# Attention state held once, scaled on ScalarE and multiplied as two 48x48 products

## The chip, the cores and the metric

The kernel runs on one core of a Trainium2 chip. The metric is device time in microseconds (us) of one execution; lower is better. TensorE is called PE below (PEld its weight loads), VectorE DVE, ScalarE ACT, GpSimd POOL, and SP is the engine that issues the DMAs. Before the change the median is 834.35 us over three runs (833.73 to 834.75).

## What is computed

The reference has three stages, each fed by the one before. Only the first is touched by the change. It is a gated linear attention over 4 batches, 8 heads, 768 tokens and 48 channels per head:

```python
f = 1.0 / (1.0 + np.exp(-f_logit))
state = np.zeros((B, H, D, D), dtype=np.float32)
for t in range(S):
    state = f[:, :, t, :, None] * state + np.einsum('bhd,bhe->bhde', k[:, :, t], v[:, :, t])
    y[:, :, t] = np.einsum('bhd,bhde->bhe', q[:, :, t], state)
```

The other two are a gated layer with a 768x768 mix over tokens (`h = relu(x @ w_in)`, normalize the second half over channels, `w_spatial @ v_n + b_spatial`, gate, `@ w_out`) and a mixer (`u = x + (relu(x.T @ w_tok1) @ w_tok2).T`, `u + relu(u @ w_ch1) @ w_ch2`). Inputs of the attention are of size 0.1 with decay logits around 2; the weights arrive as float64 or float32.

## The kernel before, in words

**Attention.** A unit (`att_unit`) is one pair of heads over half of the tokens of a batch: 4 batches x 2 halves x 4 pairs = 32 units, named batch, half, pair: unit 013 is batch 0, second half, fourth pair. The two heads of a pair lie on partitions 0 to 47 and 64 to 111. A unit has 3 chunks of 128 tokens. `chunked` (L195) works in these steps. ACT makes the decays `fs` by a sigmoid (L346). DVE copies each chunk's first decay into `first` (L202), zeroes it in `fs` (L203), scans the running decay `pc` (L204), bounds the chunk-end decays from below (L209), inverts them (L210), scans the inverse `gc` backwards (L211) and multiplies keys and queries by both (L214). POOL keeps the end decays in `pend` (L207). PE transposes the keys (L220), ACT copies them to `kn` (L222); PE makes the scores of the two heads (L229) into two PSUM tiles `pa`, ACT copies them to `am` (L233), and POOL masks them (L234). PE makes the chunk's sum of keys times values `pk` (L243, L244). DVE keeps the running state `z` of 48 columns (L265, L267), and beside it writes for each chunk but the very first a `state` (L254): `z` scaled by the end decay, set twice side by side into a 112x96 block and multiplied by a mask `own` of ones and zeros, so that the block is diagonal over the two heads. So one product of 112 rows and 112 columns serves both heads (L279); to it are added the values times the masked scores, head by head (L274, L285). There are 80 such states: 2 in each unit of a first half, 3 in each of a second. The result `py` is split into two parts of fewer bits, `xh` (ACT, L357) and `xl` (DVE, L358). The fourth pair's parts, `yh` and `yl`, are copied by 12 small DMAs (L363) into the rows that the others leave.

**Later stages.** `s1` multiplies `xh` and `xl` by w_in (through `mm3`, L130 to L132, PSUM tiles `pv` and `pu`), `s23` makes the mix over tokens (tile `ps`) and the output (`px`), phase 2 the mixer. Weights are split on the chip into two parts, piece by piece, by `split_weight`: a DMA into a ring of three buffers, then steps on DVE (L78, L81, L91), ACT (L85, L87, L92, L98) and POOL (L86, L101).

**Order.** Units are emitted step by step, each unit's first step ahead of the unit before it (`att`), and woven with the steps of `s1`, `s23` and the weights (`weave`). The tile framework then puts the instructions in order with its own scheduler, which knows of every engine, and each engine runs its queue strictly in that order. Loads and the small copies share one DMA-issuing queue, SP's. After the run, `pend`'s least value decides whether a second, general body runs; with these inputs it doesn't.

Of the kernel before, what the change touches and what calls it, by code (L numbers as in the profile page):

```python
# [8 lines left out]
F32 = mybir.dt.float32  # L9
# [9 lines left out]
def tile_kernel(ctx, tc, fkqs, v, w_in, w_sp, b_sp, w_out, w_t1, w_t2, w_c1, w_c2, out):  # L19
# [34 lines left out]
    # weights as sums of two parts of 12 bits each; float64 is rounded to float32 on the way  # L54
    LEAST = 3.4332275390625e-05 ** 2

    def split_weight(pool, stage, src, name, n, cols, eng, first=0, order=None):
        """Tiles of both parts, and the steps that fill them, piece by piece."""
        wide = src.dtype == mybir.dt.uint64
        h = pool.tile([P, n, cols], F32R, name=name + "h")  # L60
        l = pool.tile([P, n, cols], F32R, name=name + "l")
        if wide:
            src = src.bitcast(U32)
        srcr = src.rearrange("(n p) c -> n p c", p=P)

        def piece(i, c0, width):
            sl = (slice(None), i, slice(c0, c0 + width))
            at = stage.tile([P, WST], U32, tag="wsa", name=f"{name}sa{i}{c0}")
            a = at[:, :width]
            if wide:  # L70
                st = stage.tile([P, WST, 2], U32, tag="wst", name=f"{name}st{i}{c0}")
                nc.sync.dma_start(
                    out=st[:, :width, :].rearrange("p c t -> p (c t)"),
                    in_=srcr[first + i][:, 2 * c0 : 2 * (c0 + width)],
                )
                yield
                lo, hi = st[:, :width, 0], st[:, :width, 1]
                nc.vector.tensor_scalar(  # L78
                    out=a, in0=hi, scalar1=3, scalar2=0x3FFFFFFF, op0=ALU.logical_shift_left, op1=ALU.bitwise_and
                )  # L80
                nc.vector.scalar_tensor_tensor(  # L81
                    out=a, in0=hi, scalar=0xC0000000, in1=a, op0=ALU.bitwise_and, op1=ALU.bitwise_or
                )
                # the low word's first 3 bits, rounded
                nc.scalar.activation(lo, lo, AF.Copy, scale=2.0**-29)  # L85
                nc.gpsimd.tensor_tensor(out=a, in0=a, in1=lo, op=ALU.add)  # L86
                nc.scalar.activation(f32(hi), f32(hi), AF.Square)  # L87
                yield
                # zero below float32's least normal number
                a = f32(a)  # L90
                nc.vector.scalar_tensor_tensor(out=a, in0=f32(hi), scalar=LEAST, in1=a, op0=ALU.is_ge, op1=ALU.mult)  # L91
                nc.scalar.copy(h[sl], a)  # L92
                yield
            else:
                a = f32(a)
                nc.sync.dma_start(out=a, in_=srcr[first + i][:, c0 : c0 + width])
                yield
                nc.scalar.copy(h[sl], a)  # L98
                yield
                yield  # L100
            eng.tensor_tensor(out=l[sl], in0=a, in1=f32(h[sl]), op=ALU.subtract)  # L101

        where = [(i, c0, min(WST, cols - c0)) for i in range(n) for c0 in range(0, cols, WST)]
        return h, l, [partial(piece, *x) for x in (order(where) if order else where)]

    def staged(pieces):
        """Steps in which each piece is one stage behind the one after it."""
# [10 lines left out]
    def weave(main, *fillers):  # L118
        """Emit the steps of main with those of the others spread evenly before them."""
        for n, m in enumerate(main):  # L120
            for fl in fillers:
                for x in fl[len(fl) * n // len(main) : len(fl) * (n + 1) // len(main)]:
                    x()
            m()

    def mm3(ps, pairs, first=True, **kw):
        """ps += sum over (lh, ll, rh, rl) of (lh + ll)^T (rh + rl) without the product of both low parts."""
# [6 lines left out]
    def body(general):  # L134
        # ---------------- phase 1 pools
# [37 lines left out]
        first, last = (attp.tile([P, W], F32, name=x) for x in ("first", "last"))  # L173
        states = [attp.tile([P, 128], F32, name=f"state{i}") for i in range(4)]
        own = attp.tile([P, 2, D], F32, name="own")
        for t in [first, last, own] + states:
            nc.gpsimd.memset(t, 0.0)
        for j in range(2):
            nc.gpsimd.memset(own[64 * j : 64 * j + D, j, :], 1.0)
# [5 lines left out]
        cnt = {"state": 0}  # L185
# [9 lines left out]
        def chunked(u, b, hf, p, fs, fkq, vt):  # L195
            ki, qi = fkq[:, 1, :], fkq[:, 2, :]
            n0 = hf * NCW
            # decay from the chunk's start, and its inverse (from the chunk's end backwards); both scans pass
            # through all chunks and start anew where the factor is zero and the other operand is not
            pg = at2.tile([P, 2, W], F32, tag="pg", name=f"pg{u}")  # L200
            gc, pc = pg[:, 0, :], pg[:, 1, :]
            nc.vector.tensor_copy(first[:, ::C], fs[:, :W:C])  # L202
# [4 lines left out]
            nc.gpsimd.tensor_copy(pend[:, b * NP + p, n0 : n0 + NCW], pc[:, C - 1 :: C])  # L207
            ends = last[:, C - 1 :: C]
            nc.vector.tensor_scalar(out=ends, in0=pc[:, C - 1 :: C], scalar1=LOW, scalar2=None, op0=ALU.max)  # L209
            nc.vector.reciprocal(ends, ends)  # L210
# [5 lines left out]
            # keys with tokens on partitions  # L216
# [6 lines left out]
            # scores, transposed  # L223
# [15 lines left out]
            # chunk states  # L239
# [7 lines left out]
            for c in range(NCW):  # L247
                n = n0 + c
                if n > 0:
# [4 lines left out]
                    nc.vector.scalar_tensor_tensor(  # L254
                        out=now[c][:112].rearrange("p (j e) -> p j e", j=2)[:, :, :D],
                        in0=zprev[:112].unsqueeze(1).to_broadcast([112, 2, D]),
                        scalar=pp[:112],
                        in1=own[:112],
                        op0=ALU.mult,
                        op1=ALU.mult,  # L260
                    )
# [10 lines left out]
            # only a bank's first product may start afresh; where nothing was written since, the others store  # L272
# [5 lines left out]
            for c in range(now[0] is None, NCW):  # L278
                nc.tensor.matmul(  # L279
                    py[:112, c, :], now[c][:112, :112], qi[:112, c * C : (c + 1) * C],  # L280
                    start=c == 0, stop=False, skip_group_check=True,
                )
# [8 lines left out]
        def scanned(u, b, hf, p, fs, fkq, vt):  # L291
            """The recurrence itself, token by token, for one value channel of both heads after the other."""
# [36 lines left out]
        def att_unit(b, hf, p):  # L329
            """The steps of one pair of heads over half of the tokens."""  # L330
# [18 lines left out]
            # the last pair's channels fill the rows that the others leave  # L349
# [15 lines left out]
        def att(units):  # L365
            """Steps of these units in turn, the first of each ahead of the unit before it."""
# [97 lines left out]
        # ---------------- phase 1  # L464
# [44 lines left out]
        if not general:  # L509
            # does any chunk's decay come near float32's range?  # L510
# [8 lines left out]
        # ---------------- phase 2  # L519
# [70 lines left out]
        def ff(b, hf):  # L590
            """Token half hf through both channel layers; a block's second product comes after the next one's first."""
# [78 lines left out]
    # If so, all is done again in a way that holds for any decay.  # L670
# [47 lines left out]
```

## Time and profile before

| | |
|---|---|
| median of 3 runs (lowest, highest) | 834.35 us (833.73, 834.75) |
| span of the profiled execution | 835.6 us |
| PE busy | 770.3 us, 92% |
| PEld busy | 708.6 us, 85% |
| DVE busy | 462.2 us, 55% |
| ACT busy | 277.7 us, 33% |
| POOL busy | 232.9 us, 28% |

The page gives no time of the profiled execution besides its span, from the first instruction to the last; it is 1.25 us above the median of the runs. A share over the whole span says little here: attention runs in the first 370 us only, beside the loading and splitting of weights at first and beside the products of the later stages after that. In rows of the timeline a matmul's end is modelled, so only starts are subtracted from starts. A float32 product appears as two matmul records, an fp32r product (L130 to L132) as one.

### The profile page before, as it was taken

The page shows a single profiled execution, that of the slowest core. Times are in us where ns is not written, and L with a number is a line of the kernel's source. Part 1 is how long each engine was busy: PE and PEld are TensorE (multiplying, and loading weights), DVE is VectorE, ACT ScalarE, POOL GpSimd, SP SyncE. Part 2 cuts the span into 40 slices and gives each one's busy share as a digit, 9 for nine tenths or more (in the row PEclk, how much of TensorE's full clock was granted, in tenths as well). Part 3 has the DMA queues.
Part 4 walks back from the last instruction along what each step waited for, and adds up shares of the span by engine and source line. Part 5 has one row for each costly group of instructions (what it writes and reads, how often), then busy time and mean ns, then how long its engine had stood idle before and what let it go on. Part 6 is the DMA issues. An engine that isn't in the chain of part 4 may idle for free.

```text
span 835.6 us, 12502 instructions
## 1 busy us (share of the span) xinstructions
PE 770.3 (92%) x4785; PEld 708.6 (85%) x4785; DVE 462.2 (55%) x916; ACT 277.7 (33%) x590; POOL 232.9 (28%) x290
## 2 busy tenths in 40 slices
PE   3579599999999999999879889999999999999996
PEld 2357478988889878998769788999999999999995
DVE  6988977783777648638996796222122312222211
ACT  4544543333423343226645553112111311111110
POOL 5786721121112122106873661004001210001000
PEclk9999679999999999999999999999999999999998
DMA  7464321330223211203434321002000200000001
GB/s 248 128 210 131 127 93 56 129 107 33 86 77 110 91 38 57 90 20 107 153 95 130 128 72 59 21 1 86 1 29 1 86 1 28 1 1 30 14 16 34
DMA packets 30055, 61.09 MB, mean 73 GB/s; under 512 B 4128, under 2 KB 19872, under 8 KB 29984
## 3 DMA queue, kind: packets, MB, share of 16 engines
q1 hardware_dynamic: 29984, 60.18, 22.5%
q8 instruction: 40, 0.66, 0.3%
q14 instruction: 31, 0.25, 0.1%
HBM read 48.37 MB, written 9.44 MB: 69 GB/s over the span
## 4 chain that ended last, share of the span: by engine, by line
PE 71%; DVE 15%; DMA 6%; issue 4%; ACT 1%; POOL 1%; SPq 1%; DVEq 0%; ACTq 0%; POOLq 0%
PE po L615 17%; PE p L132 7%; PE p L131 7%; PE p L130 7%; PE ps L130 4%; PE ps L132 3%; PE ps L131 3%; PE pa L229 3%; PE py L285 2%; PE py L279 2%; PE px L130 2%; PE px L132 2%; PE px L131 2%; PE pv L130 2%; PE pu L130 2%
## 5 line engine op out<-in xcount | busy, mean ns | idle before, releaser
L603 DVE SCALAR_TENSOR_TENSOR hl<-p,hh 128x384 fp32r<-128x384 f32 x96 | 53.4, 557 | 176.5 <-ACT hh L602 176.5
L602 ACT ACTIVATE hh<-p 128x384 fp32r<-128x384 f32 x96 | 47.1, 491 | 183.4 <-PE p L132 183.4
L615 PE MATMUL po<-hl,wc2h 128*128 128x384 f32 x288 | 98.2, 341 | 1.4 <-DVE hl L603 1.4
L615 PE MATMUL po<-hh,wc2l 128*128 128x384 f32 x288 | 97.3, 338 | 0.0
L626 POOL TENSOR_TENSOR us<-uh,ul 128x384 f32<-128x384 f32 x24 | 25.4, 1066 | 197.6 <-DVE ul L586 180.3
L615 PE MATMUL po<-hh,wc2h 128*128 128x384 f32 x288 | 76.0, 340 | 4.0 <-ACT hh L602 4.0
L234 POOL TENSOR_SCALAR_AFFINE_SELECT am<-am 128x384 f32<-128x384 f32 x64 | 40.7, 651 | 114.8 <-ACT am L233 114.7
L130 PE MATMUL ps<-wsph,vh 128*128 128x384 f32 x192 | 67.3, 350 | 1.7 <-DVE g L439 1.7
L132 PE MATMUL ps<-wsph,vl 128*128 128x384 f32 x192 | 65.3, 343 | 0.3 <-DVE vl L412 0.3
L131 PE MATMUL ps<-wspl,vh 128*128 128x384 f32 x192 | 65.2, 340 | 0.0
L132 PE MATMUL p<-uh,wc1l 128*128 128x384 f32 x192 | 64.9, 338 | 0.0
L131 PE MATMUL p<-ul,wc1h 128*128 128x384 f32 x192 | 64.7, 337 | 0.0
L130 PE MATMUL p<-uh,wc1h 128*128 128x384 f32 x192 | 64.6, 338 | 0.1
L615 PEld LDWEIGHTS po<-hh,wc2h 128*128 128x128 f32 x288 | 52.4, 189 | 5.5 <-ACT hh L602 5.5
L615 PEld LDWEIGHTS po<-hl,wc2h 128*128 128x128 f32 x288 | 54.5, 189 | 2.7 <-DVE hl L603 2.7
L615 PEld LDWEIGHTS po<-hh,wc2l 128*128 128x128 f32 x288 | 54.5, 189 | 0.0
L279 PE MATMUL py<-fkq,state 112*112 112x128 f32 x160 | 36.1, 324 | 8.1 <-DVE state L254 6.1
L229 PE MATMUL pa<-fkq 48*128 48x128 f32 x384 | 42.5, 331 | 0.9 <-ACT am L233 0.9
L229 PEld LDWEIGHTS pa<-fkq 48*128 48x128 f32 x384 | 31.9, 217 | 10.8 <-issue 5.4
L130 PEld LDWEIGHTS ps<-wsph,vh 128*128 128x128 f32 x192 | 36.2, 188 | 5.0 <-DVE g L439 2.0
L279 PEld LDWEIGHTS py<-fkq,state 112*112 112x112 f32 x160 | 26.7, 198 | 14.9 <-DVE state L254 9.0
L130 PE MATMUL pu<-xh,winh 128*128 128x384 f32 x96 | 34.6, 361 | 5.0 <-ACT u L419 3.4
(167 smaller groups left out, 1933.6 us busy)
## 6 DMA issues: line engine op xcount, KB each, us to landing
fkq<-in_fkq SPq DMA_DIRECT2D x31, 576.0 KB, 3.8
vt<-in_v SPq DMA_DIRECT2D x8, 576.0 KB, 6.0
x1d<-xs SPq DMA_DIRECT2D x24, 192.0 KB, 1.9
xf<-x1d SPq DMA_DIRECT2D x12, 384.0 KB, 4.5
wc2st<-in_w_c SPq DMA_DIRECT2D x12, 384.0 KB, 3.2
out<-ot SPq DMA_DIRECT2D x24, 192.0 KB, 2.0
wc1st<-in_w_c SPq DMA_DIRECT2D x8, 384.0 KB, 3.8
winst<-in_w_in SPq DMA_DIRECT2D x6, 384.0 KB, 4.1
```

The lines of the kernel that those rows point to most:

```text
L130: nc.tensor.matmul(ps, lh, rh, start=first and i == 0, stop=False, **kw)
L131: nc.tensor.matmul(ps, lh, rl, start=False, stop=False, **kw)
L132: nc.tensor.matmul(ps, ll, rh, start=False, stop=i == n - 1, **kw)
L229: nc.tensor.matmul(pa[j][:, c, :], ki[64 * j : 64 * j + D, sl], qi[64 * j : 64 * j + D, sl], start=True, stop=True)
L234: nc.gpsimd.affine_select(out=am[j], in_=am[j], compare_op=ALU.is_ge, fill=0.0, base=0, pattern=[[0, NCW], [1, C]], channel_multiplier=-1,)
L279: nc.tensor.matmul(py[:112, c, :], now[c][:112, :112], qi[:112, c * C : (c + 1) * C], start=c == 0, stop=False, skip_group_check=True,)
L285: nc.tensor.matmul(py[64 * j : 64 * j + m, c, :], vt[:, c, h0 + D * j : h0 + D * j + m], am[j][:, c, :], start=False, stop=True, skip_grou ...
L602: nc.scalar.activation(hh, ps, AF.Relu)
L603: nc.vector.scalar_tensor_tensor(out=hl, in0=ps, scalar=0.0, in1=f32(hh), op0=ALU.max, op1=ALU.subtract)
L615: nc.tensor.matmul(po[c], l[:, ft, csl], r, start=ft == 0 and x == 0, stop=ft == NF - 1 and x == 2)
L626: nc.gpsimd.tensor_tensor(out=us[c], in0=f32(uh[:, c, tsl]), in1=f32(ul[:, c, tsl]), op=ALU.add)
```

## The change

The state is held once, 48 columns wide, in six tiles of 64 columns whose last 16 stay zero, and is scaled by ACT. The product with the queries becomes two, one for each head, of 48 rows and 64 or 48 columns. The mask `own` goes. `first` has two tiles, and ACT fills it by a sigmoid of the chunk's first logits, beside the one that makes `fs`. `pend` is copied by ACT. The end decays are inverted without the bound from below. Lines after L202 move up by 2 to 9; comments are taken out, which moves nothing.

```diff
-        first, last = (attp.tile([P, W], F32, name=x) for x in ("first", "last"))
-        states = [attp.tile([P, 128], F32, name=f"state{i}") for i in range(4)]
-        own = attp.tile([P, 2, D], F32, name="own")
-        for t in [first, last, own] + states:
+        firsts = [attp.tile([P, W], F32, name=f"first{i}") for i in range(2)]
+        last = attp.tile([P, W], F32, name="last")
+        states = [attp.tile([P, 64], F32, name=f"state{i}") for i in range(6)]
+        for t in firsts + [last] + states:
             nc.gpsimd.memset(t, 0.0)
-        for j in range(2):
-            nc.gpsimd.memset(own[64 * j : 64 * j + D, j, :], 1.0)
...
-            nc.vector.tensor_copy(first[:, ::C], fs[:, :W:C])
+            first = firsts[cnt["unit"] % 2]
+            cnt["unit"] += 1
+            nc.scalar.activation(first[:, ::C], fkq[:, 0, ::C], AF.Sigmoid)
             nc.vector.memset(fs[:, ::C], 0.0)
...
-            nc.gpsimd.tensor_copy(pend[:, b * NP + p, n0 : n0 + NCW], pc[:, C - 1 :: C])
-            ends = last[:, C - 1 :: C]
-            nc.vector.tensor_scalar(out=ends, in0=pc[:, C - 1 :: C], scalar1=LOW, scalar2=None, op0=ALU.max)
-            nc.vector.reciprocal(ends, ends)
+            nc.scalar.copy(pend[:, b * NP + p, n0 : n0 + NCW], pc[:, C - 1 :: C])
+            nc.vector.reciprocal(last[:, C - 1 :: C], pc[:, C - 1 :: C])
...
-                    nc.vector.scalar_tensor_tensor(
-                        out=now[c][:112].rearrange("p (j e) -> p j e", j=2)[:, :, :D],
-                        in0=zprev[:112].unsqueeze(1).to_broadcast([112, 2, D]),
-                        scalar=pp[:112],
-                        in1=own[:112],
-                        op0=ALU.mult,
-                        op1=ALU.mult,
-                    )
+                    nc.scalar.activation(now[c][:112, :D], zprev[:112], AF.Copy, scale=pp[:112])
...
             for c in range(now[0] is None, NCW):
-                nc.tensor.matmul(
-                    py[:112, c, :], now[c][:112, :112], qi[:112, c * C : (c + 1) * C],
-                    start=c == 0, stop=False, skip_group_check=True,
-                )
+                for j, m in ((0, 64), (1, D)):
+                    r = slice(64 * j, 64 * j + D)
+                    nc.tensor.matmul(
+                        py[64 * j : 64 * j + m, c, :], now[c][r, :m], qi[r, c * C : (c + 1) * C],
+                        start=c == 0, stop=False, skip_group_check=True,
+                    )
```

The scheduler then orders each engine's instructions anew. Three places follow.

On PE, unit 110's products of state and queries (its tile `py110`; `ps011` is the mix of batch 0). Before:

```order
L131 MATMUL ps011_1541<-wspl_498,vh0_501 128x384
L279 MATMUL py110_1483<-fkq110_1291,state1_125 112x128
L132 MATMUL ps011_1541<-wsph_497,vl0_502 128x384
L279 MATMUL py110_1483<-fkq110_1291,state2_126 112x128
L285 MATMUL py110_1483<-am1100_1440,vt11_1295 64x128
L285 MATMUL py110_1483<-am1101_1441,vt11_1295 48x128
```

Now:

```order
L132 MATMUL ps011_1559<-wsph_503,vl0_508 128x384
L272 MATMUL py110_1499<-fkq110_1307,state5_130 64x128
L272 MATMUL py110_1499<-fkq110_1307,state5_130 48x128
L130 MATMUL ps011_1559<-wsph_503,vh0_507 128x384
L131 MATMUL ps011_1559<-wspl_504,vh0_507 128x384
L132 MATMUL ps011_1559<-wsph_503,vl0_508 128x384
L272 MATMUL py110_1499<-fkq110_1307,state0_125 64x128
L272 MATMUL py110_1499<-fkq110_1307,state0_125 48x128
L278 MATMUL py110_1499<-am1100_1456,vt11_1311 64x128
```

Where a product of full height stood between other full-height products, two of 48 rows stand between them.

On ACT, the copy of unit 003's result, `yh003`, from which the first DMAs into `xh00` are made (`wsph` is a piece of the mix's weights, `wspsa` its load). Before:

```order
L98 CAST wsph_497<-wspsa20_604 128x384
L98 CAST wsph_497<-wspsa2384_627 128x384
L357 CAST yh003_479<-py003_461 112x384
L98 CAST wsph_497<-wspsa30_655 128x384
L222 COPY kn011_609<-pt011_606 128x224
```

Now:

```order
L98 CAST wsph_503<-wspsa20_610 128x384
L98 CAST wsph_503<-wspsa2384_633 128x384
L252 ACTIVATE state3_128<-z0100_572,pend_64 112x48
L252 ACTIVATE state4_129<-z0101_575,pend_64 112x48
L98 CAST wsph_503<-wspsa30_664 128x384
L350 CAST yh003_485<-py003_465 112x384
```

`yh003` now stands behind the piece `wsph` of the load `wspsa30`, and behind two states.

On ACT, the same copy at the end of batch 0, `yh013` (`wt1st` are loads of w_t1, `vh0` and `u00` tiles of `s1`). Before:

```order
L411 CAST vh0_501<-vf002_765 128x512
L87 ACTIVATE wt1st00_3930<-wt1st00_3930 128x256
L357 CAST yh013_881<-py013_864 112x384
L92 CAST wouth_499<-woutsa30_1101 128x384
```

Now:

```order
L252 ACTIVATE state1_126<-z0131_880,pend_64 112x48
L85 ACTIVATE wt1st10_4004<-wt1st10_4004 128x256
L220 COPY kn100_984<-pt100_980 128x336
L92 CAST wouth_505<-woutsa30_1114 128x384
L231 COPY am1000_988<-pa1000_986 128x384
L231 COPY am1001_989<-pa1001_987 128x384
L207 COPY pend_64<-pg101_972 128x3
L87 ACTIVATE wt1st10_4004<-wt1st10_4004 128x256
L85 ACTIVATE wt1st20_4030<-wt1st20_4030 128x256
L350 CAST yh013_895<-py013_875 112x384
```

Between the state that unit 013's last product needs and the copy of its result there now stand eight instructions, among them the conversion of the load `wt1st20`, which before came after `yh013`.

## Rows read from the trace of the kernel before

**Rows 1.** Windows: stretch in us; its length, busy of PE, PEld, DVE, ACT, POOL; PEclk, DMA

```profile
0.00:62.90 62.90, 33.55 (x234) 25.31 (x234) 53.82 (x106) 29.95 (x67) 43.46 (x60) 1.00 0.63 195
62.90:104.70 41.80, 32.25 (x206) 24.48 (x205) 37.65 (x79) 20.33 (x47) 27.88 (x30) 0.82 0.41 130
104.70:113.40 8.70, 8.69 (x30) 6.74 (x31) 5.87 (x13) 3.54 (x9) 2.22 (x5) 0.50 0.53 174
113.40:370.00 256.60, 256.60 (x1862) 223.04 (x1860) 172.50 (x413) 90.56 (x198) 46.85 (x94) 1.00 0.23 74
370.00:835.00 465.00, 439.22 (x2460) 428.99 (x2458) 192.32 (x308) 133.32 (x271) 112.50 (x101) 0.98 0.15 49
```

**Rows 2.** Chain that ended last, 94 to 106 us: start, us, what

```profile
95.31 0.59 DVE state L254
95.94 0.77 PE py L279 x2
...
98.23 0.48 ACT yh L357
...
99.80 4.78 DMA xh<-yh
...
104.71 0.77 PE pv L130
```

**Rows 3.** Timeline of PE at unit 110's products: start, us, line, tiles, records

```profile
152.25 0.38 PE L279 MATMUL py<-fkq,state 112*112 112x128 f32 x2
152.39 0.42 PE L132 MATMUL ps<-wsph,vl 128*128 128x384 f32 x1
152.66 0.38 PE L279 MATMUL py<-fkq,state 112*112 112x128 f32 x2
152.97 0.87 PE L285 MATMUL py<-am,vt 128*64 128x128 f32 x12
153.76 0.45 PE L130 MATMUL ps<-wsph,vh 128*128 128x384 f32 x1
154.05 0.34 PE L131 MATMUL ps<-wspl,vh 128*128 128x384 f32 x1
154.22 0.35 PE L132 MATMUL ps<-wsph,vl 128*128 128x384 f32 x1
...
155.75 0.94 PE L229 MATMUL pa<-fkq 48*128 48x128 f32 x12
156.90 0.34 PE L131 MATMUL px<-woutl,gh 128*128 128x384 f32 x1
```

**Rows 4.** Timeline of PE, a shorter run of the same products

```profile
122.81 0.65 PE L285 MATMUL py<-am,vt 128*64 128x128 f32 x8
123.39 0.44 PE L130 MATMUL pu<-xh,winh 128*128 128x384 f32 x1
```

**Rows 5.** Groups by line and shape: count, busy us, mean ns, idle before

```profile
L254 DVE SCALAR_TENSOR_TENSOR state<-z,pend,own 112x96 f32<-112x96 f32 x80 | 31.2, 391 | 3.9 <-PE py L279 2.6
L209 DVE TENSOR_SCALAR last<-pg 128x3 f32<-128x3 f32 x32 | 9.6, 301 | 0.7
L202 DVE COPY first<-fs 128x3 f32<-128x3 f32 x32 | 5.7, 177 | 34.8 <-ACT fs L346 34.7
L207 POOL COPY pend<-pg 128x3 f32<-128x3 f32 x32 | 12.0, 376 | 67.4 <-DVE pg L204 67.4
L222 ACT COPY kn<-pt 128x336 f32<-128x336 f32 x16 | 7.0, 434 | 4.5 <-PE pt L220 4.5
L222 ACT COPY kn<-pt 128x224 f32<-128x224 f32 x16 | 5.5, 346 | 10.4 <-PE pt L220 10.4
```

**Rows 6.** Timelines of SP and ACT at the first copies into xh

```profile
54.14 0.33 SPq L96 DMA_DIRECT2D wspsa<-in_w_sp  x1
...
54.62 0.47 ACT L357 CAST yh<-py 112x384 fp32r<-112x384 f32 x1
56.56 0.51 ACT L98 CAST wsph<-wspsa 128x384 fp32r<-128x384 f32 x1 [1.46 <-DMA wspsa<-in_w_sp]
```

More of the change, by code (lines that the diff above doesn't have):

```diff
@@ L184, in body @@
             nc.gpsimd.memset(pick[64 : 64 + D, D + 64 : D + 65], 1.0)
-        cnt = {"state": 0}
+        cnt = {"state": 0, "unit": 0}
         zst = {}
```

## The prediction

> **What bounds the kernel now.** I read the windows by stage first, then the chain of waits, then the timeline of PE. The windows [rows 1] show three stages in which attention runs. Up to 62.9 us DVE is busy 53.8 us and PE 33.6: DVE's queue carries the start. From 62.9 to 104.7 DVE is busy 37.7 of 41.8 and PE 32.3, so DVE still leads. From 104.7 to 370 PE has work in every microsecond, at half the granted clock up to 113.4 and at the full one after. The reader should see that the 55% of DVE over the span says nothing: DVE matters only before 104.7, PE only after. The chain [rows 2] shows how the one hands over to the other: a state by DVE at 95.31, the product that waits for it at 95.94, ACT's copy of unit 013's result at 98.23, its DMAs into `xh` (4.78 us), and the first product of `s1` on batch 0's second half at 104.71. After that no row of the chain is anything but PE until the attention is done. What comes after 370 is not touched; its weight buffers take the room of the attention's, so it starts as much earlier or later as the attention ends.
>
> So the change takes work from DVE, which pays only before 104.7, and asks PE for more, which costs only after. The two have to be weighed.
>
> **PE after 104.7: the products.** In this stretch stand 58 of the 80 products of state and queries. One now costs 0.23 us: from 152.25 to 152.66 are 0.41, with one full-size product of about 0.175 in it [rows 3]. In its place come two of 48 rows, each of two records. Nothing in the trace is a product of 48 rows into 64 columns. Nearest above: each of the two costs what the one cost, 0.23, as if they ran one after the other; that adds 58 x 0.23 = 13.3 us. Nearest below: one record's 0.0525 for each of the two passes, the heads side by side, 0.105 in all, which saves 58 x 0.125 = 7.3. I take the rate of the small products: L285 needs 0.79 us for 12 records and 0.58 for 8 [rows 3, 4], so 0.0525 a record and 0.21 for four; L229, the nearest in rows used, has the same rate (below). That is 58 x 0.02 = **1.2 us less**.
>
> **PE after 104.7: the changes of form.** The rows show that full-height products follow each other freely, `L279` between fp32r products too, but that a change to a small form costs. L285 starts 0.31 us after L279, which is 0.08 over its 0.23. Its 12 records take 0.79 for 0.63 at the steady rate, 0.16 more, and the second full-size product starts 0.29 after the first where 0.17 is usual [rows 3]. The run of 8 has the same 0.16 over its 0.42 [rows 4]. I put 0.05 of it on the way in and 0.11 on the way out: 0.13 for a change into a 64-column form, 0.22 for one into a full form. The run of L229 takes 1.15 us from its first record to the second full-size product; less 0.63 for its records and 0.17 that leaves 0.35, of which 0.22 are the way out; with an entry like L285's 0.08 ahead of it a change into the 48-row, 128-column form costs 0.20 to 0.21.
>
> I counted the changes in PE's order from the first product at 104.7 to the attention's last. Before: 84 into a full form, 38 into L229's, 57 into 64 columns, 179 in all. Now: 76, 52 and 105, of which 44 are into the new form; 233 in all. The reason is the first place shown of the order: a product that stood among full ones without a toll now pays twice. At 0.22, 0.20 and 0.13 that is 33.5 us before and 40.8 now, **7.3 more**. (The same counting with all products at their steady rates gives 257 us for the stretch, where the trace has 265, 4.4 of them lost to the half clock, so it holds to some 2%.) In the new order 2 full-size products, 6 score products and some 9 small ones of this stretch stand ahead of it, while PE waits for the DMAs; at 0.17, 0.11 and up to 0.07 each that is **1.6 less**. Sum for PE: 7.3 - 1.2 - 1.6 = **+4.5 us**.
>
> A rule speaks against the products. The Trainium skill, "TensorEngine Tiling (Array Packing)", section "Restrictions and Gotchas", has it that different row tiles cannot access the same PSUM bank at the same time. Here both heads write one bank, while the pair of L229 writes two tiles; no row shows row tiles on one bank. By the rule the sum would take the upper price, +13.3 in place of -1.2.
>
> **DVE, ACT and POOL.** DVE loses L254 (391 ns), L209 (301) and L202 (177) [rows 5]. Before 104.7 these are 22, 10 and 11 instructions, 8.6 + 3.0 + 1.9 = 13.5 us; that is the most that the start can gain, and nothing is the least. After 104.7 they are hidden behind PE and are worth nothing. POOL loses 32 copies of 376 ns, some 10 of them before 104.7; POOL is busy 43.5 of the first 62.9 us, so this helps the weight pieces a little and I give it nothing of its own. ACT gets 64 instructions of 3 columns and 80 of 48. Its copies of 336 and 224 columns take 434 and 346 ns, so 0.17 us and 0.8 ns a column: 0.17 and 0.21. Before 104.7 that is some 8 us beside 50 busy ones of 104.7: room enough, but each stands in a queue that runs in order. `first` now waits for ACT where it waited for DVE, at like cost.
>
> **How much of the 13.5 arrives.** Two places of the order decide it. At the first copies into `xh00`, SP issues a load at 54.14, ACT copies `yh003` at 54.62 and turns the load that was just issued at 56.56 [rows 6]. Now `yh003` stands behind that piece. If the loads go out 3.5 us sooner, because POOL's pieces follow DVE's, the piece ends at 57.07 - 3.5 and the copy 0.5 later, at 54.1, against 55.1: one microsecond of gain, not five. At the end of the half the same happens. DVE reaches unit 013's last state some 3 us sooner by its shorter queue, and ACT makes it without DVE's other work in between, so the product at 95.94 comes to about 91. But `yh013` now waits for `wt1st20`. That load needs a buffer which DVE's last piece of w_out frees right after the state, at about 91.5; a load takes 2.4 us from issue to ACT in [rows 6], this larger one say 3.2, and its 256 columns 0.4 on ACT, so `yh013` starts at about 95.2 against 98.23. So I take **3.0 us** of gain at 104.71, an estimate from these rows, between the ends of 0 and 13.5.
>
> **Sum.** +4.5 - 3.0 = +1.5 us. The profiled execution's span of 835.6 would become 837.1; it is 1.25 above the median, and the difference is carried over to that: 834.35 + 1.5, rounded up to **836.0 us** for tolls that DVE's relief cannot hide. A measurement of this kernel tells about 0.2% from no change, 1.7 us.
>
> **Rivals.**
> *The start's gain arrives (faster).* If `yh013` does not wait for the load, two thirds of the 13.5 come through, 9 us, against +4.5 on PE: 829.9; all of it gives 825.4. For it: DVE is busy 90% of 62.9 to 104.7 [rows 1]. Against it: both copies stand behind loads. It decides once the first product of `s1`'s second half starts before 100.2. If PE then idles less, the half clock from 104.7 to 113.4 may not come, worth 8.7 / 2 = 4.4 us more.
> *Small forms change freely among themselves (faster).* 55 of the changes now are between the new form and another small one, 49 of them into 64 columns. Without their toll, 49 x 0.13 + 6 x 0.20 = 7.6 us, PE comes to -3.1 and the time to 828. Against it: the run of L229 pays on its way out as L285 does.
> *The two heads run one after the other (slower).* In `py` both write one bank. PE comes to +4.5 + 1.2 + 13.3 = +19.0 and the time to 850.4. It decides if four records take more than 0.3 us. Against it: nothing but the pair of L229, on two banks.
> *Nothing arrives at the start (slower).* The DMAs leave no gain: 838.9.
>
> **How the numbers follow.** Forecast, 832 to 840, with the last rival as its upper half: 0.55, of which 0.30 lies above 836.0, 0.25 within 0.2%. Gain at the start 0.17 and free changes 0.13, both faster. One after the other 0.15, slower, and partly so it lies at 840 to 850. So faster 0.30, same 0.25, slower 0.45. The range takes the two faster cases down to 827 and the slow one up to 846, which leaves out a full gain below and a full serial price above, together 2 in 10.
>
> **What would show it.** In the profile after: DVE without the three groups, some 46 us less; L272 in 320 records. The steps are right if four records of L272 in a row take about 0.21 us, if the first full-size product after them comes 0.3 after the one before it, if PE is busy throughout from the first product of `s1`'s second half (at 101 to 102 us) to the attention's end, and that stretch is 4 to 5 us longer. They are wrong if that first product moves by more than 5 us or not at all, if the tolls are not there, or if PE waits for ACT's states after 113.

## The result, and the profile after

| | before | after |
|---|---|---|
| median (lowest, highest; runs) | 834.39 us (833.73, 834.75; 4) | 845.50 us (843.86, 852.45; 4) |
| ratio, 95% interval | | 1.0147 [1.0107, 1.0187] |
| span of the profiled execution | 835.6 us | 842.4 us |
| PE busy | 770.3 us | 781.2 us, 93% |
| DVE, ACT, POOL busy | 462.2, 277.7, 232.9 us | 430.2, 307.6, 227.7 us |

The kernel became 11.1 us slower: inside the range and on the forecast side, but seven times the forecast's 1.6. The two profiled executions lie only 6.8 us apart, since that of before was one of the slower of its kernel and that of after one of the faster: in the other thirteen traces the span is 1.7 to 1.8 us under the time of its execution, so that of before took an estimated 837.4 us, 3.0 above its median, while that of after took 844.15, 1.35 under its own. So 4.3 of the 11.1 us stand in no trace. The spread of the four runs after, 8.6 us, stays unexplained.

The windows of the changed kernel answer to [rows 1]. Columns: stretch in us; its length, busy of PE, PEld, DVE, ACT, POOL; PEclk, DMA share, GB/s. The stretches are cut at the same places of the program: first product of `s1`, first product of its second half, end of the half clock, end of the attention.

```profile
0.00:61.60 61.60, 33.80 (x257) 23.84 (x257) 47.79 (x82) 35.66 (x98) 42.78 (x54) 1.00 0.64 201
61.60:106.90 45.30, 36.05 (x253) 26.66 (x253) 35.28 (x66) 24.61 (x67) 29.81 (x30) 0.81 0.39 125
106.90:110.20 3.30, 3.30 (x11) 2.46 (x9) 1.24 (x3) 0.58 (x2) 0.00 (x0) 0.50 0.51 135
110.20:378.70 268.50, 268.50 (x1970) 223.77 (x1968) 153.25 (x314) 113.92 (x298) 42.18 (x74) 1.00 0.23 73
```

PE is still busy in every microsecond of the last two. The attention ends 8.7 us later than before, 378.45 against 369.78 by the last product's start, and what follows gives 1.9 back, which no step of the change explains: it takes 463.8 to 467.8 us in the fourteen traces. From the first product of `s1`'s second half to there it was 265.1 us, now it is 271.5; but before, 8.7 of them ran at half clock and now only 3.3. So at full clock it is 260.7 against 269.9: **9.2 us more work on PE**, where 4.5 were forecast. That first product came 2.2 us later, at 106.94, where 3.0 sooner was forecast.

**Where PE's time went.** Timelines of PE, then of its weight loads, at the place of [rows 3], unit 110's products (start, us, line, tiles, records):

```profile
149.99 0.34 PE L132 MATMUL ps<-wsph,vl 128*128 128x384 f32 x1
150.25 0.43 PE L272 MATMUL py<-fkq,state 48*64 48x128 f32 x4
150.61 0.44 PE L130 MATMUL ps<-wsph,vh 128*128 128x384 f32 x1
150.89 0.34 PE L131 MATMUL ps<-wspl,vh 128*128 128x384 f32 x1
...
151.33 0.43 PE L272 MATMUL py<-fkq,state 48*64 48x128 f32 x4
151.69 0.87 PE L278 MATMUL py<-am,vt 128*64 128x128 f32 x12
152.49 0.45 PE L130 MATMUL ps<-wsph,vh 128*128 128x384 f32 x1
```

```profile
149.81 0.19 PEld L132 LDWEIGHTS ps<-wsph,vl 128*128 128x128 f32 x1
150.25 0.19 PEld L272 LDWEIGHTS py<-fkq,state 48*64 48x64 f32 x4 [0.25 <-issue]
150.61 0.19 PEld L130 LDWEIGHTS ps<-wsph,vh 128*128 128x128 f32 x1 [0.17 <-issue]
150.72 0.19 PEld L131 LDWEIGHTS ps<-wspl,vh 128*128 128x128 f32 x1
```

From 149.99 to 150.89 are two full products (0.35 at their steady rate) and one pair of small ones: 0.55 for the pair, where the one product cost 0.23. The weight loads show why. Between products of one form the next weights are loaded while a product runs: L131's at 150.72 under L130's product of 150.61. At a change of form the load stands still for 0.25 or 0.17 us and starts only with the product that needs it. In the rest of the stretch it is the same: before a load that follows one of another form the loads stand still for 0.05 to 0.37 us, 0.17 on the mean of 231, and before one of the same form for at most 0.10 (1714 loads).

The second place is the scores. The rows are PE's timeline after, two units on:

```profile
154.46 0.94 PE L227 MATMUL pa<-fkq 48*128 48x128 f32 x12
155.33 0.44 PE L130 MATMUL px<-wouth,gh 128*128 128x384 f32 x1
...
160.84 0.93 PE L227 MATMUL pa<-fkq 48*128 48x128 f32 x10
161.70 0.65 PE L272 MATMUL py<-fkq,state 48*64 48x128 f32 x8
162.28 0.87 PE L278 MATMUL py<-am,vt 128*64 128x128 f32 x12
163.08 0.49 PE L227 MATMUL pa<-fkq 48*128 48x128 f32 x2
163.49 0.26 PE L241 MATMUL pk<-vt,kn 128*64 128x48 f32 x1
```

A unit's 12 score records take 0.87 us in one piece (154.46 to 155.33). Where the small products break in, 10 take 0.86 and the last 2 another 0.41. Ten cost as much as twelve because a head's product without the other head's beside it takes the time of both: the records of a pair start 7 ns apart and the next pair 0.11 us later, and the last two records of the ten, of one head, start at 161.39 and 161.50. I call such a piece, with an odd number of products, an odd one.

**Where the start went.** PE's timeline around unit 013's product, which answers to [rows 2], and ACT's before its copy:

```profile
93.14 0.68 PE L272 MATMUL py<-fkq,state 48*64 48x128 f32 x4 [2.60 <-DVE xl L351]
94.07 1.28 PE L272 MATMUL py<-fkq,state 48*64 48x128 f32 x8 [0.26 <-ACT state L252]
95.28 1.54 PE L278 MATMUL py<-am,vt 128*64 128x128 f32 x12
...
100.94 0.79 PE L218 MATMUL pt<-ident,fkq 112*128 112x112 f32 x3 [3.50 <-issue]
101.66 1.65 PE L227 MATMUL pa<-fkq 48*128 48x128 f32 x12
...
106.94 0.80 PE L130 MATMUL pv<-winh,xh 128*128 128x512 f32 x1
```

```profile
94.29 0.32 ACT L252 ACTIVATE state<-z,pend 112x48 f32<-112x48 f32 x1
...
97.60 0.20 ACT L207 COPY pend<-pg 128x3 f32<-128x3 f32 x1 [1.16 <-DVE pg L204]
97.91 0.43 ACT L87 ACTIVATE wt1st<-wt1st 128x256 f32<-128x256 f32 x1
98.25 0.42 ACT L85 ACTIVATE wt1st<-wt1st 128x256 uint32<-128x256 uint32 x1
98.57 0.46 ACT L350 CAST yh<-py 112x384 fp32r<-112x384 f32 x1
```

The weight load of the unit's third product, and PE's row of its first product before the change:

```profile
94.67 0.28 PEld L272 LDWEIGHTS py<-fkq,state 48*64 48x64 f32 x4 [0.32 <-ACT state L252]
```

```profile
90.40 0.77 PE L279 MATMUL py<-fkq,state 112*112 112x128 f32 x2 [1.93 <-DVE xl L358]
```

The unit's first product did not wait for its state but, 2.60 us, for DVE to empty `py` of unit 012; it came at 93.14, before the change at 90.40. The second and third, at 94.07 and 94.67, then waited shortly for ACT, which made the last state at 94.29. The copy of their result stood on ACT behind `pend` of unit 101, which now makes ACT wait 1.16 us for DVE's scan, and behind two conversions. Then unit 101's transposes and scores and unit 100's results stand ahead of `s1`'s product on PE, for 6.0 us at half clock.

The new and remaining groups of ACT and PE, as in [rows 5]:

```profile
L252 ACT ACTIVATE state<-z,pend 112x48 f32<-112x48 f32 x80 | 25.7, 332 | 32.7 <-DVE z L258 14.2 <-DVE z L256 9.5 <-PE py L272 7.6
L207 ACT COPY pend<-pg 128x3 f32<-128x3 f32 x32 | 6.3, 196 | 17.7 <-DVE pg L204 17.6
L202 ACT ACTIVATE first<-fkq 128x3 f32<-128x3 f32 x32 | 6.2, 194 | 0.0
L272 PE MATMUL py<-fkq,state 48*64 48x128 f32 x160 | 34.7, 321 | 3.9 <-DVE xl L351 2.6 <-ACT state L252 1.3
L272 PE MATMUL py<-fkq,state 48*48 48x128 f32 x160 | 33.7, 314 | 0.0
```

The three groups of DVE, 46.5 us, are gone, though DVE's busy time fell by only 32.0: records of DVE overlap, and others of them take longer. Of PE's two groups, only 3.9 us of idle time stand ahead, and none of it after 106.9.

### The profile page after: what moved, and what is told of

It reads as the page before. It is cut to its first block, busy times and chain, and to the rows that moved or that the text cites. A ratio compares the mean times of both kernels' runs of the same rounds, so it can differ in the third digit from the quotient of the medians.

```text
span 842.4 us, 12829 instructions
## 1 busy us (share of the span) xinstructions
PE 781.2 (93%) x4945; PEld 707.5 (84%) x4945; DVE 430.2 (51%) x772; ACT 307.6 (37%) x734; POOL 227.7 (27%) x258
## 4 chain that ended last, share of the span: by engine, by line
PE 76%; DVE 11%; issue 4%; DMA 3%; POOL 2%; ACT 1%; SPq 1%; DVEq 0%; POOLq 0%; ACTq 0%
PE po L608 17%; PE p L132 7%; PE p L131 7%; PE p L130 7%; PE ps L130 4%; PE pa L227 4%; PE ps L131 4%; PE ps L132 3%; PE py L272 3%; PE py L278 2%; PE px L130 2%; PE px L132 2%; PE px L131 2%; PE pv L130 2%; PE pv L131 1%
## 5 line engine op out<-in xcount | busy, mean ns | idle before, releaser
L232 POOL TENSOR_SCALAR_AFFINE_SELECT am<-am 128x384 f32<-128x384 f32 x64 | 46.0, 732 | 179.3 <-ACT am L231 179.3
L130 PE MATMUL ps<-wsph,vh 128*128 128x384 f32 x192 | 67.2, 350 | 1.4 <-DVE g L432 1.3
L131 PE MATMUL ps<-wspl,vh 128*128 128x384 f32 x192 | 65.3, 340 | 0.0
L131 PE MATMUL p<-ul,wc1h 128*128 128x384 f32 x192 | 65.1, 339 | 0.0
L130 PE MATMUL p<-uh,wc1h 128*128 128x384 f32 x192 | 64.9, 340 | 0.0
L227 PE MATMUL pa<-fkq 48*128 48x128 f32 x384 | 48.3, 335 | 0.0
L227 PEld LDWEIGHTS pa<-fkq 48*128 48x128 f32 x384 | 35.6, 219 | 12.1 <-issue 8.1
L130 PE MATMUL pu<-xh,winh 128*128 128x384 f32 x96 | 35.1, 366 | 8.2 <-ACT r L390 4.1
L130 PEld LDWEIGHTS ps<-wsph,vh 128*128 128x128 f32 x192 | 36.1, 188 | 5.2 <-issue 1.7
L272 PE MATMUL py<-fkq,state 48*48 48x128 f32 (+1 forms) x320 | 34.7, 317 | 3.9 <-DVE xl L351 2.6
L130 PE MATMUL px<-wouth,gh 128*128 128x384 f32 x96 | 34.4, 360 | 3.5 <-DVE g L432 2.5
```

Of the source, the lines that this page charges most:

```text
L130: nc.tensor.matmul(ps, lh, rh, start=first and i == 0, stop=False, **kw)
L131: nc.tensor.matmul(ps, lh, rl, start=False, stop=False, **kw)
L227: nc.tensor.matmul(pa[j][:, c, :], ki[64 * j : 64 * j + D, sl], qi[64 * j : 64 * j + D, sl], start=True, stop=True)
L232: nc.gpsimd.affine_select(out=am[j], in_=am[j], compare_op=ALU.is_ge, fill=0.0, base=0, pattern=[[0, NCW], [1, C]], channel_multiplier=-1,)
L272: nc.tensor.matmul(py[64 * j : 64 * j + m, c, :], now[c][r, :m], qi[r, c * C : (c + 1) * C], start=c == 0, stop=False, skip_group_check=True,)
```

## The experiments

The kernels built on the change leave out the bound of the end decays, as it does. A product's form is its number of rows (48, or 112 and more) and of columns (64 and less, or 112 and more); with both the larger it is full. "Changes" are changes of form counted in PE's records from the first product of `s1`'s second half to the end of the attention.

**1 to 4: which part of the change costs?** One product with all else of the change (`e1`):

```diff
-                    nc.scalar.activation(now[c][:112, :D], zprev[:112], AF.Copy, scale=pp[:112])
+                    for j in range(2):
+                        r = slice(64 * j, 64 * j + D)
+                        nc.scalar.activation(now[c][r, 64 * j : 64 * j + D], zprev[r], AF.Copy, scale=pp[r])
...
-                for j, m in ((0, 64), (1, D)):
...
+                nc.tensor.matmul(
+                    py[:112, c, :], now[c][:112, :112], qi[:112, c * C : (c + 1) * C],
+                    start=c == 0, stop=False, skip_group_check=True,
+                )
```

> The change with the product put back: ACT writes the two heads' blocks into a 128-column state (two activations in place of one) and one product of 112 rows serves both heads; all that the change moved to ACT stays there. Theory A (the 9 us that PE lost between the first product of s1's second half and the end of the attention come from the small products: more changes of form, and scores of the two heads split from each other by them): in this kernel's order PE changes form 187 times there (179 before, 233 in the change) and 20 pieces of scores hold an odd number of products (14 and 34), so this stretch is 1 to 2 us longer than before, and the time is 833 to 838. Theory B (the loss comes from ACT: states and end decays in its queue, whatever the product): the time stays at 842 to 848, since ACT has 80 more activations still.

Two products in the kernel before (`e2`), the state scaled by DVE:

```diff
-                    nc.vector.scalar_tensor_tensor(
-                        out=now[c][:112].rearrange("p (j e) -> p j e", j=2)[:, :, :D],
...
+                    nc.vector.tensor_scalar(
+                        out=now[c][:112, :D], in0=zprev[:112], scalar1=pp[:112], scalar2=None, op0=ALU.mult
+                    )
```

> The kernel before with the two 48x48 products alone: six states of 64 columns, scaled by DVE (one tensor_scalar of 112x48), the bound, the first decays and pend where they were. Theory A: 213 changes of form and 28 odd pieces of scores in the stretch, which with the gaps measured in the two traces make it about 4 us longer than before; 836 to 842. Theory B: PE loses little without ACT's new work; 832 to 836.

The change with that `tensor_scalar` on DVE in place of ACT's activation (`e3`):

> The change with the state scaled by DVE in place of ACT; all else of it stays. Theory A: 222 changes of form and 22 odd pieces, so the stretch is about 5 us longer than before and 4 shorter than in the change; 838 to 843. Theory B (the states on ACT are what costs): 832 to 836, as before.

The change with the states and the product of before (`e4`):

> The kernel before with the decays' part alone: first decays by a sigmoid on ACT into two tiles, pend copied by ACT, no bound; the state stays DVE's block diagonal one with one product. Theory A: 186 changes of form and 12 odd pieces, so PE's stretch is within 1 us of before, and what is left is the start: 0 to 3 us sooner, 831 to 836. Theory B: copies in ACT's queue cost too, 836 to 840.

Measured: `e1` 836.9 us, ratio 1.0011 [0.9991, 1.0030]; `e2` 846.8, 1.0113 [1.0081, 1.0145]; `e3` 844.5, 1.0085 [1.0059, 1.0112]; `e4` 834.8, 0.9978 [0.9962, 0.9994]. With one product the loss is gone although ACT has 80 more activations than in the change; with two products it is there without any of ACT's work. Theory B falls in all four. Theory A held for `e1` and `e4`; `e2` came out 5 us above its range and `e3` 1.5. PE's stretch answers for 5 us of each, at full clock (table below); the rest is the start: PE idles 36.4 and 35.2 us ahead of the stretch, against 31.3 before, in `e2` mostly ahead of the states' products (14.8 us, against 8.1 before). Whether ACT or DVE does the scaling (`e3` against the change) stays open: the intervals, of different sessions, just overlap, and `e3`'s stretch is 4.4 us shorter with 12 changes and 12 odd pieces less.

**5 to 8: is it the number of pieces?** The scores get a higher priority, nothing else, in the change (`e5`), in the kernel before (`e6`), in `e4` (`e7`) and in `e1` (`e8`):

```diff
-            for c in range(NCW):
-                for j in range(2):
+            with tc.high_priority(300):
+                for c in range(NCW):
+                    for j in range(2):
```

> The change, with the scores of a unit (tile pa) emitted at a higher priority, so that the scheduler keeps a unit's six score products in one piece; nothing else. In its order, between the first product of s1's second half and the attention's end, PE changes form 170 times (234 in the change), no piece of scores holds an odd number of products (34 in the change), and the states' products come in 32 pieces (44). Theory A (the loss is the number of pieces, with the gaps of the two traces: 0.21 us a piece into a full form or of scores, 0.15 a piece of the others, 0.11 an odd piece): that stretch becomes some 15 us shorter than in the change and 7 shorter than before; with the start as it is in the change the time is 827 to 833. Theory C (a product of 48 rows costs more than its records show, wherever it stands): the 116 products stay dear, and the time stays above 838.

> The kernel before with the same priority for the scores: 152 changes of form (180 before), no odd piece (14). Theory A: some 5 us less on PE, 828 to 833. Theory C: no difference to before, 834 to 837.

> The decays' part alone (first decays and pend on ACT, no bound; state by DVE, one product) with the same priority for the scores: 149 changes of form, no odd piece. Theory A: some 8 us less on PE than before, 826 to 831, faster than the change with whole scores by the difference of 21 changes. Theory C: as the decays' part alone, 833 to 837.

> The change with one product (states' blocks by two activations on ACT) and the same priority for the scores: 143 changes of form, no odd piece. Theory A: some 9 us less on PE than before, 825 to 830; the least of the four, 2 to 3 us under the change with whole scores. Theory C: as with one product alone, 835 to 838.

Measured: `e5` 832.5 us, 0.9972 [0.9952, 0.9992]; `e6` 830.3, 0.9941 [0.9924, 0.9958]; `e7` 827.1, 0.9904 [0.9873, 0.9934]; `e8` 827.2, 0.9902 [0.9878, 0.9926]. All four lie in theory A's ranges. The change lost its whole loss, 13 us, with its 320 small records untouched: its stretch is the window

```profile
109.93:366.10 256.17, 256.17 (x1978) 219.08 (x1978) 156.38 (x321) 109.64 (x298) 43.93 (x74) 0.99 0.24 77
```

against 271.5. Theory C falls: what the small products cost hangs on the changes around them. One side forecast missed: `e8` was to be the least of the four, 2 to 3 us under `e5`. It is 5.3 under, and level with `e7`; at full clock its stretch is 1.3 us shorter than that of `e5`, and it begins 5.4 sooner.

**9: many pieces without the small products.** `e1` with the transposes in the priority too, which makes the scheduler break the scores up.

```diff
+            with tc.high_priority(300):
+                for c in range(ncs):
+                    nc.tensor.transpose(pt[:, c, :], ki[:112, c * C : (c + 1) * C], ident[:112, :112])
```

> The change with one product (as in the first run: no product of 48 rows for the states), and with transposes and scores both emitted at a higher priority, which makes the scheduler break the scores up: in its order between the first product of s1's second half and the attention's end PE changes form 232 times (187 with one product alone, 233 in the change), and 44 pieces of scores hold an odd number of products (20 and 34). Theory A (the number of pieces sets the time; a fit to the ten traces so far gives 0.15 us a change and 0.19 an odd piece): that stretch is 45 x 0.15 + 24 x 0.19 = 11 us longer than with one product alone, so 844 to 852, as slow as the change, without a small product for the states. Theory C (the small products themselves are dear): 835 to 838, as with one product alone.

Measured: 850.2 us, 1.0189 [1.0156, 1.0222], at least as slow as the change (1.0147 [1.0107, 1.0187]). Its PE timeline at one unit, where `e1` has one piece of 12 records in 0.87 us:

```profile
177.07 0.32 PE L219 MATMUL pt<-ident,fkq 112*128 112x112 f32 x1
177.32 0.48 PE L229 MATMUL pa<-fkq 48*128 48x128 f32 x2
177.73 0.31 PE L219 MATMUL pt<-ident,fkq 112*128 112x112 f32 x1
177.98 0.48 PE L229 MATMUL pa<-fkq 48*128 48x128 f32 x2
178.39 0.31 PE L219 MATMUL pt<-ident,fkq 112*128 112x112 f32 x1
178.64 0.71 PE L229 MATMUL pa<-fkq 48*128 48x128 f32 x8
179.28 0.45 PE L130 MATMUL ps<-wsph,vh 128*128 128x384 f32 x1
```

The 12 records and two of the transposes take from 177.32 to 179.28, 1.96 us, for 0.83 at their steady rates (0.63 and 0.20). So the number of pieces is enough to make the loss, and the two small products of the state are not needed for it.

**10 to 12: what is the start worth?** In `e10` unit 101's products and unit 100's results are queued behind `s1`'s first product on PE:

```diff
+            if key and i == 0:
+                hold[key] = x.ins
...
+            with tc.issue_after(hold["s1"]):
```

> The change, with unit 101's transposes, scores and results and unit 100's results held on PE behind the first product of s1's second half. Theory D (the start of that product is what the start is worth): it comes 2 us sooner than in the change, at 104 to 105, and the time falls by as much, to 842 to 844. Theory E (what counts is the time that PE stands idle before the attention's end; work ahead of that product only fills it): the product comes sooner, but PE waits longer for xh ahead of it and does the held pieces after it, with 251 changes of form in place of 234; 845 to 850, no gain.

In `e11` the conversions of w_t1 on ACT are queued behind unit 013's copy in the same way, and in `e12` this is added to `e8`:

> The change, with ACT's conversions of the pieces of w_t1 held behind the copy of unit 013's result. The prediction's reason for a small gain (that copy waits for the load of a w_t1 piece): the copy comes 1 to 2 us sooner, so do xh's transfers and the first product of s1's second half, and the time falls to 842 to 844. Theory E: on PE unit 101's pieces still stand ahead of that product and end at about 107, so PE idles as long as in the change; what is left are 8 changes of form less (226), 1 to 2 us: 843 to 846.

> The change with one product and whole scores, and w_t1's conversions behind unit 013's copy. Theory E: PE idles there only for unit 101's scores (3.9 us before) and the changes of form stay at 143; 826 to 828, no difference to whole scores with one product. The prediction's reason: 1 to 2 us less, 825 to 826.

Measured: `e10` 848.7 us, 1.0168 [1.0137, 1.0198]; `e11` 843.7, 1.0107 [1.0077, 1.0138]; `e12` 826.0, 0.9894 [0.9864, 0.9924]. The row of `e10`:

```profile
102.47 0.76 PE L132 MATMUL pv<-winh,xh 128*128 128x512 f32 x1 [5.51 <-DMA xh<-yh]
```

`s1`'s product came 4.5 us sooner than in the change, more than either theory said, and the attention ended 2.9 us later than there: theory D falls. PE now waits 5.51 us for the DMAs where it waited 3.50 for unit 101, and does that work afterwards. Of the 7.2 us by which its stretch is longer at full clock, 2.4 are this work at its steady rates; 17 more changes and 4 more odd pieces are 3.6 by the fit below, so the run does not show what an earlier start is worth with as many changes. The rows of `e11`, ACT's copy and PE:

```profile
96.70 0.48 ACT L356 CAST yh<-py 112x384 fp32r<-112x384 f32 x1 [0.67 <-PE py L284]
```

```profile
99.99 0.79 PE L224 MATMUL pt<-ident,fkq 112*128 112x112 f32 x3 [2.73 <-issue]
...
105.99 0.80 PE L136 MATMUL pv<-winh,xh 128*128 128x512 f32 x1
```

The copy came 1.9 us sooner, as the prediction's reason has it, `s1`'s product 0.95. Its time lies in the range of both theories, and 8 changes less are in it, so this run does not tell them apart; nor do `e12`'s 1.2 us under `e8`, whose intervals overlap.

**All fourteen together.** From each trace: the changes; the odd pieces of scores; the stretch from `s1`'s second half to the attention's end, less half of its time at half clock; what is left of that when each product is taken off at the rate that it has among its like (full-size 0.174 us, of 512 columns 0.226; a record of a small product 0.053, of L279 0.113, of a transpose 0.10, of `pk` 0.03); and 0.19 times the changes plus 0.08 times the odd pieces, the best fit of two numbers (0.192 and 0.084, unrounded). The last column is PE's idle time ahead of the stretch, from its first product on. There PE ran at half clock for 39 to 59 us in the traces of `e3`, `e5`, `e7` and `e11` and for 13 to 21 in the others, so in this column those four are not to be compared with the rest.

| kernel | changes | odd | stretch | left | fit | idle ahead |
|---|---|---|---|---|---|---|
| before | 179 | 14 | 260.7 | 35.8 | 35.5 | 31.3 |
| the change | 233 | 34 | 269.9 | 47.4 | 47.6 | 29.8 |
| `e1` one product | 186 | 20 | 262.2 | 37.9 | 37.4 | 29.6 |
| `e2` two products alone | 212 | 28 | 265.8 | 43.2 | 43.1 | 36.4 |
| `e3` states on DVE | 221 | 22 | 265.5 | 43.2 | 44.3 | 35.2 |
| `e4` decays alone | 185 | 12 | 262.6 | 37.7 | 36.5 | 33.7 |
| `e5` whole scores, the change | 169 | 0 | 254.4 | 31.6 | 32.5 | 34.7 |
| `e6` whole scores, before | 151 | 0 | 255.2 | 28.0 | 29.0 | 37.6 |
| `e7` whole scores, `e4` | 148 | 0 | 253.5 | 29.1 | 28.4 | 31.3 |
| `e8` whole scores, `e1` | 142 | 0 | 253.1 | 27.6 | 27.3 | 31.7 |
| `e9` many pieces, `e1` | 231 | 44 | 271.3 | 47.3 | 48.0 | 24.7 |
| `e10` PE's order | 250 | 38 | 277.1 | 52.3 | 51.2 | 31.8 |
| `e11` ACT's order | 225 | 34 | 268.1 | 45.7 | 46.0 | 29.1 |
| `e12` `e8`, ACT's order | 142 | 0 | 253.9 | 27.5 | 27.3 | 32.7 |

Two numbers give 14 kernels over a range of 25 us, to 1.2 us each. With a number of their own, the changes to or from a full form (125 to 227) come to 0.193 us each and those between two small forms (4 to 85) to 0.189. The odd pieces rise and fall with the changes, so their price is the less certain: 0.08, give or take 0.03. (The expectation of `e9` has 0.15 and 0.19; a fit of the first ten traces gives these if a constant is left free beside the two.)

## Why the prediction was wrong in size

The forecast had the sign, since PE loses more than the start can give. That the time lies in the range was luck: the range above 840 was there for the two heads one after the other, which did not happen.

- **What bounds the kernel** held in the main: DVE leads up to 61.6 us, PE after 106.9 (between them DVE is busy 35.3 us and PE 36.1), and no state on ACT is waited for after 106.9.
- **The products** (1.2 us less) held. Eight records of L272 take 0.58 us (161.70 to 162.28) and four 0.36 (150.25 to 150.61), so four more cost 0.22; 0.21 was forecast.
- **The changes of form** failed, as the term that was mis-sized: 7.3 us forecast. Their number was right, 179 and 233 in the traces too. Their price was not: 0.13 had been put on a change into a 64-column form, from the way that L285 is entered from L279, a full form [rows 3]. Among full forms the prices held: the pair of small products takes 0.55 us, 0.34 over its 0.21, for 0.13 + 0.22. But 58 of the changes now lead into one of 64 columns from another small form, where 6 did. There the rows after have 0.36 us from four records of L272 to the first of L278 (151.33 to 151.69), 0.15 over their steady 0.21, and L278 then still pays its own way in. At the 0.19 of the fit the 54 changes are 10.4 us. And a cost was not in the sum at all: 20 more odd pieces, 1.7 us by the fit. Together 12.1.
- **Work moved ahead** (1.6 less) held: products at steady rates are 2.5 us less in the stretch, 0.8 of it from the products' own price.
- **Half clock**: the forecast said 4.4 us could be had only if the start's gain arrived. 2.7 of it came without, since the half clock ended at 110.2, 3.3 us into the stretch (8.7 before); ahead of the stretch PE ran at half clock for 2.0 us more. 12.1 - 2.5 - 2.7 = 6.9, where the stretch grew by 6.4.
- **The start** (3.0 less at the first product of `s1`'s second half) failed in sign at that product, and the step that failed is which wait comes last. The forecast let unit 013's third product, at 95.94 before, come at about 91; it came at 94.67, since the first stood until 93.14 behind the emptying of `py` and the last two states came from ACT only then. It let the copy wait for a load; `pend`'s wait for DVE on ACT's queue, a wait that the change adds, did that first. And it took off 1.6 us for work done ahead of that product and 3.0 for its earlier start, though the one delays the other: in `e10`, with unit 101's work behind it, the product came 4.5 us sooner and the end 2.9 later. In the trace PE's first product starts 0.3 us sooner and PE idles 1.5 less ahead of the stretch (29.8 against 31.3), but it is busy 4.1 longer there, so the stretch begins 2.2 later. The 4.1 are, as an estimate, 10 more changes of form (64 against 54; 1.9 by the fit), 1.0 of products moved ahead, and 1.0 for the half clock.
- **The rivals.** That small forms change freely among themselves falls by the rows above and by the 0.189 us of the fit: it is among them that the price was highest against the forecast. That the two heads run one after the other falls: four records more cost 0.22 us, and in the records the second head's product starts 7 ns after the first's. That nothing arrives at the start is nearest to what happened; with PE's measured 9.2 in place of its 4.5 it would have given 843.6. The rule of the Trainium skill, "TensorEngine Tiling (Array Packing)", "Restrictions and Gotchas", that row tiles cannot access one PSUM bank at the same time, would have cost 14.5 us here, by the prediction's prices. The trace does not agree with it for two heads that write different partitions of the bank: their starts lie 7 ns apart.
- **ACT's price** was off without effect: a state takes 332 ns, where 0.21 us was taken from the copies of 336 and 224 columns.

The rule that mattered stands on the same page of the Trainium skill, under "Tiling Modes", "Key Properties": changing the tiling mode drains the engine. The trace agrees, with weight loads idle for 0.17 us on the mean of 231 changes, and the fourteen traces give 0.19 us a change. That the drain is what holds the loads back was not tested by itself.

## What to carry to other kernels

On a full PE, cost small products by the changes of form that they bring and by the runs of other small products that they break up, not by their own time: count the pieces in the new order before and after. Keep the pieces whole: giving a unit's scores a higher priority was worth 5 to 13 us in each of the four versions tried, and `e12` (one product, states and decays on ACT, whole scores, 826.0 us) beats the kernel before by 1.1% and, by the medians, the change by 2.3%. And do not price a start by when a certain instruction begins: `e10` has it 4.5 us sooner and ends later. Take the idle and the busy time of the engine that bounds what follows, both of them: `e9` idles least ahead of the stretch, 24.7 us, and begins it 1.6 us later than the change, with 81 changes of form before it where the change has 64.

## What was not expected of the hardware

- A product of one head alone takes PE as long as the two heads' side by side: 10 score records 0.86 us, 12 records 0.87, 2 records 0.41.
- A change between two small forms costs about as much as one from a full form: 0.193 us with a full form in it, 0.189 between two small ones, over the fourteen kernels.
- Two products of 48 rows that write different partitions of one PSUM tile, `py`, run side by side: they start 7 ns apart, and four more records cost 0.22 us.
